# Converting a weight quarter one matmul group later: VectorE's half of the work and the reload behind it, in the last round of a routed expert layer

## The chip, the core and the metric

The kernel runs on one core of a Trainium2 chip. The metric is the device time of one execution in microseconds (us). The engines are TensorE (PE in the profile, its weight loads PEld), VectorE (DVE), ScalarE (ACT), GpSimd (POOL) and SyncE (SP), which issues most of the DMAs. A "q" behind an engine's name (DVEq) is its sequencer.

## What is computed

A Fourier transform over two axes, and then a layer of 8 experts of which each row uses one:

```python
X = np.fft.fft(np.fft.fft(x, axis=1), axis=2).real      # x: 8 x 2496 x 256
x = X.reshape(19968, 256)
logits = x @ w_gate                                     # 8 experts
e_idx = np.argmax(logits, axis=1)                       # one expert per row
gate_w = softmax(logits)[row, e_idx]
eom = sigmoid(x @ w_output_gate)
for e in range(8):
    mask = e_idx == e
    h = np.maximum(x[mask] @ w1[e], 0.0)                # 256 -> 1024
    ye = h @ w2[e]                                      # 1024 -> 256
    out[mask] = gate_w[mask, None] * eom[mask, e, None] * ye
```

Nothing is known of the routing when the kernel is built; which rows go to which expert is worked out on the chip.

## The kernel before

The transform comes first, with the gate behind it; each row is written to a scratch array `scr`, sorted by expert. Then the expert part runs over a list of slots, `sched`. Rounds 0 to 2 hold 512 rows of each expert in two slots of 256 rows, and they run while the transform of later batches goes on. The last round (`LAST`, the subject here, about 715 to 1068 us of the profiled execution) holds what is left: 27 "pair" slots of 256 rows, and 10 "single" slots of 128 rows interleaved with them. Which expert a slot of the last round has is a number in a table, read into a register when the slot comes up.

Numbers are held as sums of two 16-bit values, high and low, so each product takes three matmuls. Of a slot, four groups `g` are worked: `mm1` (line 1325, 12 matmuls into the PSUM tile `hp`, which has three buffers), then ScalarE's `hh` (line 1329, the high part of the hidden layer, and the relu), then VectorE's `hl` (line 1330, the low part, which reads `hp` and `hh`), then `mm2` of the group three earlier (line 1347, into `yp`). `hp` comes free when `hl` has read it. With `mm2` of group 2 VectorE makes `ysc` (line 1352), with that of group 3 ScalarE makes `y` (line 1355), and GpSimd scatters it (line 1356).

The weights of an expert come in four quarters: two halves of w1 (`raw0b` in 32 bit, `w0b` converted) and two of w2 (`raw1b`, `w1b`). Conversion is done by `conv`: ScalarE writes the high part (line 1300), VectorE the low part (line 1302, which reads the high one), and SyncE then issues the load of the next expert's quarter into the same raw buffer (`load_w`, line 1272, behind two register loads at line 1233). Pair slots have one set of buffers, single slots another. In the last round a pair slot whose expert is that of the slot before skips the conversion, by a branch (`tc.If`, line 1298) on a register, and skips the load's transfer by a condition on the DMA; single slots always convert.

The order on each engine is the order in which the code is written. In `experts` a slot begins with `load_x_` for the slot after next (on SyncE: `xr`, line 1255, a transposing DMA, and `xf`, line 1256). Then, for each group, `mm1`, `mm2` of the group three earlier, and conversions: the new expert's halves of w1 at groups 1 and 3 of the pair slot before it, those of w2 at groups 0 and 2 of the slot that follows. A single slot's quarters are converted from a list, `todo`, one at a time, as soon as their buffers are free.

`final` is filled when the last round's tables are ready, towards the end of round 2; from there on the order is that of the code alone.

Of the kernel before, what the change touches and what calls it, by code (L numbers as in the profile page):

```python
# [245 lines left out]
def fft_moe_kernel(ctx: ExitStack, tc: tile.TileContext, xl, wg, w1, w2, tde, tdo, gt, ts0, tsm, tsr, tsq, cst, tid, out):  # L246
# [47 lines left out]
    if True:  # L294
# [108 lines left out]
        newest, pinned, final = {}, [], []  # L403
        evacs = {}

        def behind_rows(eng, on=True):
            return tc.issue_after(evacs[eng]) if on else nullcontext()
# [773 lines left out]
    if True:  # L1181
# [25 lines left out]
        NS = len(sched)  # L1207
# [5 lines left out]
        after_new = dict(zip(news, news[1:]))  # L1213
# [3 lines left out]
        after_sing = dict(zip(sing, sing[1:]))  # L1217

        def chained(fn, n, *args):
            if n < NS:  # L1220
                fn(n, *args)
# [3 lines left out]
        def table(n):  # L1225
            rd, qi = sched[n][:2]
            return (slots_a + [slots_b, fbt])[rd], (E, NQ, NFB)[max(rd, LAST - 1) - LAST + 1], 0 if rd == FB else qi
# [56 lines left out]
        def changed(n):  # L1284

            if n not in fresh:
                t, w, qi = table(n)
                need(sched[n][0])
                fresh.clear()
                fresh[n] = nc.values_load(t[0:1, 2 * w + qi:2 * w + qi + 1], engines=CONV, min_val=0, max_val=1)  # L1290
            return fresh[n]

        def conv(n, m, h):
            rd, qi, N, wb, _, _ = sched[n]
            r, w = raw[wb][m][h], wbuf[wb][m][h]
            sc = scale_of(n, m)
            skips = wb == 0 and rd == LAST
            with tc.If(changed(n) > 0) if skips else nullcontext():  # L1298
                with behind_rows("ACT", not n):
                    nc.scalar.activation(w[:, 0], r, AF.Copy, scale=sc)  # L1300
                with behind_rows("DVE", not n):
                    nc.vector.scalar_tensor_tensor(w[:, 1], r, sc, w[:, 0], op0=ALU.mult, op1=ALU.subtract)  # L1302
            nxt = (after_new if wb == 0 else after_sing).get(n, NS)
            if n:
                chained(load_w, nxt, m, h)
            else:
                late.append((nxt, m, h))

        def halves(a, h):
            for k in ("hh", "hl"):  # L1310
                a[k, h] = fx[0].tile([128, 4, 256], F16, name=k, tag=k, bufs=3)

        def mm1(n, g):
            a = sl_[n]
            T = slice(0, a["N"])
            if g % 2 == 0:
                halves(a, g // 2)
            w1v = wbuf[a["wb"]][0][g // 2].rearrange("p a (k f) -> p a k f", k=2)
            ps = psf["h"].tile([128, 2, 256], F32, name="hp", tag="h", bufs=psf["hb"])
            for k in range(2):  # L1320
                f = 2 * g + k
                m = 0
                for kc in range(2):
                    for hl, x in ((0, kc), (0, 2 + kc), (1, kc)):
                        nc.tensor.matmul(ps[:, k, T], w1v[:, hl, kc, (f % 4) * 128:(f % 4 + 1) * 128], a["x"][:, x, T], start=(m == 0), stop=(m == 5))  # L1325
                        m += 1
            G = slice(2 * (g % 2), 2 * (g % 2) + 2)
            hh, hl = a["hh", g // 2], a["hl", g // 2]
            i = nc.scalar.activation(hh[:, G, T], ps[:, :, T], AF.Relu)  # L1329
            j = nc.vector.scalar_tensor_tensor(hl[:, G, T], ps[:, :, T], 0.0, hh[:, G, T], op0=ALU.max, op1=ALU.subtract)  # L1330
            if sched[n][0] < LAST and not final:
                newest.update(ACT=getattr(i, "ins", i), DVE=getattr(j, "ins", j))

        def mm2(n, g):
            a = sl_[n]
            U, h = a["U"], g // 2
            M = min(128, a["N"])
            w2v = wbuf[a["wb"]][1][h].rearrange("p a (f d) -> p a f d", f=4)
            if g == 0:
                a["yp"] = psf["h"].tile([128, 2, 256], F32, name="yp", tag="y", bufs=psf["yb"])  # L1340
                a["y"] = fx[0].tile([128, 2, 256], F32, name="y", tag="y", bufs=2)
                a["ys"] = fx[0].tile([128, 2], F32, name="ysc", tag="ysc", bufs=2)
            u = g % 2 if U == 2 else 0
            for f in range(4) if U == 2 else range(2 * (g % 2), 2 * (g % 2) + 2):
                for m, (k, hl) in enumerate((("hh", 0), ("hh", 1), ("hl", 0))):

                    nc.tensor.matmul(a["yp"][0:M, u], a[k, h][:, f, u * 128:u * 128 + M], w2v[:, hl, f],  # L1347
                                     start=(g == 0 and f == 0 and m == 0), stop=(h == 1 and f == 3 and m == 2), skip_group_check=U == 2)
            ys = a["ys"]
            if g == 2:  # L1350
                with behind("DVE"):
                    nc.vector.tensor_scalar(ys[:, 0:U], a["f"][:, 0:U, 0], scale_of(n, 2), None, op0=ALU.mult)
            if g == 3:
                for u in range(U):
                    nc.scalar.activation(a["y"][0:M, u], a["yp"][0:M, u], AF.Copy, scale=ys[0:M, u:u + 1])  # L1355
                    put = nc.gpsimd.indirect_dma_start(  # L1356
                        out=out[:, :], out_offset=bass.IndirectOffsetOnAxis(ap=a["f"].bitcast(I32)[0:M, u, 1:2], axis=0),
                        in_=a["y"][0:M, u], in_offset=None, bounds_check=NTOK - 1, oob_is_err=False)
                    if sched[n][0] < FB:
                        free_order("out", put)  # L1360
                del sl_[n]

        fbt = fbs = None

# [42 lines left out]
        late = []  # L1407

        def experts():
            yield "w"  # L1410
            chained(load_x_, 0)
            hold.clear()
            chained(load_x_, 1)
            for a in late:
                load_w(*a)
            yield "i"
            todo = []
            for n in range(NS + 1):
                chained(load_x_, n + 2)
                if n == sing[0] - 4:  # L1420
                    for m in range(2):
                        for h in range(2):
                            load_w(sing[0], m, h)
                if n + 3 in sing:
                    todo += [(n + 3, m, h) for m in range(2) for h in range(2)]
                for g in range(4):
                    if n < NS:
                        mm1(n, g)
                        yield "h"

                    k, j = divmod(4 * n + g - LAG, 4)
                    if 0 <= k < NS:
                        mm2(k, j)
                        yield "y"

                    nb, k_ = next_sq.get(n, (0, 0))
                    if nb:
                        for what in SQ[4 * k_ + g]:
                            if what[1] is None:
                                wscale(sched[nb][1], what[0])  # L1440
                            else:
                                wenergy(nb, *what)

                    p = n - 1 + g % 2
                    if p in next_new:
                        conv(next_new[p], (g + 1) % 2, g // 2)
                    if todo:
                        k, m, h = todo[0]

                        prev = ([-9] + sing)[sing.index(k)]  # L1450
                        if 4 * n + g >= 4 * prev + 2 * h + 1 + LAG * m:
                            conv(*todo.pop(0))
                yield ("slot", n)
            spill = nc.values_load(more[0:1, 0:1], min_val=0, max_val=1)
            with tc.If(spill > 0):  # L1455
                for n in range(NS, len(sched)):
                    load_x_(n)
                    for m in range(2):
                        for h in range(2):
                            load_w(n, m, h)  # L1460
                    for h in range(2):
                        conv(n, 0, h)
                    for g in range(4):
                        mm1(n, g)
                    for h in range(2):
                        conv(n, 1, h)
                    for g in range(4):
                        mm2(n, g)
            short = nc.values_load(more[0:1, 1:2], min_val=0, max_val=1)
            with tc.If(short > 0):  # L1470
                general()
# [40 lines left out]
    def need(i):  # L1512
        while min(i, LAST) not in ready:
            next(bg, None)
# [73 lines left out]
```

## Time and profile before

| what | value |
|---|---|
| median of three runs | 1077.16 us (1074.88 to 1079.08) |
| the profiled execution | 1077.15 us, span 1075.3 us, mean granted clock 0.987 |
| TensorE busy | 1031.2 us, 96% of the span |
| VectorE busy | 668.1 us, 62% |
| ScalarE busy | 597.5 us, 56% |
| GpSimd busy | 422.8 us, 39% |
| DMA | 170.96 MB, mean 159 GB/s |

The span is what the profile covers; 1.85 us of the profiled execution lie around it. A busy share is a mean over the transform, the early rounds and the last round, which have different limits, so for the change the stretch from 715 to 1034 us is read by itself. An instruction with a bracket at its end, as [2.13 <-DVE hl L1330], found its engine idle for so long, and was released by what stands behind the arrow. A matmul group is 12 matmuls on one line.

### The profile page before, as it was taken

To read this page: it belongs to the slowest core of one execution; us is meant where nothing else is said; L and a number is where in the kernel's file an instruction comes from. 1 tells how busy PE (TensorE), PEld (TensorE's weight loads), DVE (VectorE), ACT (ScalarE), POOL (GpSimd) and SP (SyncE) were. 2 spreads that over 40 slices of the span, in tenths; PEclk is the share of its full clock that TensorE was granted. 3 is DMA by queue.
4 is the path that set the end of the run, shared out by engine and by line. 5 is a ranking of instruction groups with operands and counts; after the bars stand their busy time and mean duration, and the time that the engine had idled before them with its cause. 6 is when DMAs were issued, how large, how long until landed. Compare 5 with 4: busy or idle time off the path is not lost. (4 is left out here: it accounts for less than half of the span.)

```text
span 1075.3 us, 27862 instructions
## 1 busy us (share of the span) xinstructions
PE 1031.2 (96%) x10179; PEld 911.9 (85%) x10179; DVE 668.1 (62%) x1381; ACT 597.5 (56%) x1099; POOL 422.8 (39%) x384
## 2 busy tenths in 40 slices
PE   8888889999999999999999999999999999999997
PEld 6676768889889889988888888888999889988996
DVE  5989787786876585566586444544535455445542
ACT  3476756776775465656544555444545555445652
POOL 0068355755574572353357752221122121212121
PEclk8998989999999999999999999999999999999999
DMA  9642565675686265566556885635737766475830
GB/s 365 204 175 83 199 167 166 194 197 138 157 206 157 76 163 141 139 168 167 145 132 172 211 206 149 158 104 139 194 74 202 167 168 131 124 202 129 194 74 24
DMA packets 152312, 170.96 MB, mean 159 GB/s; under 512 B 115309, under 2 KB 116207, under 8 KB 152164
## 3 DMA queue, kind: packets, MB, share of 16 engines
q1 hardware_dynamic: 136292, 126.48, 47.2%
q0 software_dynamic: 15728, 42.14, 11.6%
q8 instruction: 82, 1.34, 0.6%
q10 hardware_dynamic: 144, 0.46, 0.2%
q14 instruction: 66, 0.54, 0.2%
HBM read 149.45 MB, written 43.63 MB: 180 GB/s over the span
## 5 line engine op out<-in xcount | busy, mean ns | idle before, releaser
L1325 PE MATMUL hp<-xr,w0b 128*128 128x256 f16 (+2 forms) x4080 | 477.4, 267 | 8.7 <-DVE hl L1330 6.9
L1347 PE MATMUL yp<-w1b,hh 128*128 128x256 f16 x2560 | 437.9, 273 | 0.0
L1325 PEld LDWEIGHTS <-w0b 128*128 128x128 f16 x4080 | 378.6, 98 | 59.8 <-issue 13.7
L1356 POOL DMA_INDIRECT out_dram<-y,xf x160 | 181.2, 1133 | 438.9 <-ACT y L1355 390.1
L1347 PE MATMUL yp<-w1b,hl 128*128 128x256 f16 x1280 | 348.9, 273 | 0.0
L1330 DVE SCALAR_TENSOR_TENSOR hl<-hp,hh 128x512 f16<-128x512 f32 (+2 forms) x340 | 221.3, 653 | 186.1 <-ACT hh L1329 162.2
L1329 ACT ACTIVATE hh<-hp 128x512 f16<-128x512 f32 (+2 forms) x340 | 192.0, 567 | 232.1 <-PE hp L1325 229.5
L1347 PEld LDWEIGHTS <-hh 128*128 128x128 f16 x2560 | 247.3, 98 | 29.9 <-issue 0.8
L749 POOL DMA_INDIRECT scr<-rows,desti x160 | 178.5, 1115 | 186.3 <-ACT rows L746 79.1
L1347 PEld LDWEIGHTS <-hl 128*128 128x128 f16 x1280 | 125.3, 98 | 14.4
L1302 DVE SCALAR_TENSOR_TENSOR w0b<-raw0b,wsc,w0b 128x1024 f16<-128x1024 f32 x44 | 60.2, 1369 | 61.5 <-ACT w0b L1300 60.4
L1355 ACT ACTIVATE y<-yp,ysc 128x256 f32<-128x256 f32 (+1 forms) x160 | 67.6, 470 | 44.0 <-PE yp L1347 34.0
L1302 DVE SCALAR_TENSOR_TENSOR w1b<-raw1b,wsc,w1b 128x1024 f16<-128x1024 f32 x44 | 57.7, 1312 | 49.5 <-ACT w1b L1300 47.1
L1300 ACT ACTIVATE w0b<-raw0b,wsc 128x1024 f16<-128x1024 f32 x44 | 50.3, 1145 | 38.8 <-PE hp L1325 37.6
L523 PE MATMUL psb_t<-tdet,ft 128*125 128x290 f32 (+1 forms) x200 | 56.2, 433 | 10.3 <-DVE ft L480 4.4
L1300 ACT ACTIVATE w1b<-raw1b,wsc 128x1024 f16<-128x1024 f32 x44 | 50.4, 1147 | 18.7 <-PE yp L1347 12.3
L523 PEld LDWEIGHTS psb_t<-tdet,ft 128*125 128x125 f32 (+1 forms) x200 | 38.7, 200 | 25.9 <-issue 8.0
L1302 DVE SCALAR_TENSOR_TENSOR w1b<-raw1b,ssc,w1b 128x1024 f16<-128x1024 f32 x32 | 41.0, 1282 | 24.6 <-ACT w1b L1300 21.1
L1302 DVE SCALAR_TENSOR_TENSOR w0b<-raw0b,ssc,w0b 128x1024 f16<-128x1024 f32 x32 | 40.8, 1282 | 21.9 <-ACT w0b L1300 21.2
L1300 ACT ACTIVATE w0b<-raw0b,ssc 128x1024 f16<-128x1024 f32 x32 | 36.3, 1144 | 14.5 <-DMA raw0b<-in_w_dram 13.4
L1300 ACT ACTIVATE w1b<-raw1b,ssc 128x1024 f16<-128x1024 f32 x32 | 36.6, 1145 | 9.9 <-DMA raw1b<-in_w_dram 6.7
L536 DVE SCALAR_TENSOR_TENSOR alo<-psb_t,p_x,ahi 125x580 f16<-125x580 f32 (+1 forms) x40 | 32.1, 817 | 15.3 <-ACT ahi L535 15.3
(232 smaller groups left out, 954.7 us busy)
## 6 DMA issues: line engine op xcount, KB each, us to landing
raw0b<-in_w_dram SPq DMA_DIRECT2D x118, 512.0 KB
raw1b<-in_w_dram SPq DMA_DIRECT2D x118, 512.0 KB
xt<-in_xl_dram SPq DMA_DIRECT2D x40, 512.0 KB
scr<-rows,desti POOLq DMA_INDIRECT x160, 3.9
out_dram<-y,xf POOLq DMA_INDIRECT x160, 3.5
xr<-scr SPq DMA_TRANSPOSE x85
xf<-scr SPq DMA_DIRECT2D x75, 2.0 KB
tst<-in_ts_dram SPq DMA_DIRECT2D x2, 512.0 KB
```

The costliest lines, as they stand in the source:

```text
L523: nc.tensor.matmul(o[:, 0:290], ft[:, k, par, W], tdab[:, k], start=(k == 0), stop=(k == 1))
L536: nc.vector.scalar_tensor_tensor(s["alo"][W, c], ps[W, :, 0:290], sc, s["ahi"][W, c], op0=ALU.mult, op1=ALU.subtract)
L749: free_order("scr", batch=b, inst=nc.gpsimd.indirect_dma_start(out=scr[:, :], out_offset=bass.IndirectOffsetOnAxis(ap=s["desti"][:, j:j + ...
L1300: nc.scalar.activation(w[:, 0], r, AF.Copy, scale=sc)
L1302: nc.vector.scalar_tensor_tensor(w[:, 1], r, sc, w[:, 0], op0=ALU.mult, op1=ALU.subtract)
L1325: nc.tensor.matmul(ps[:, k, T], w1v[:, hl, kc, (f % 4) * 128:(f % 4 + 1) * 128], a["x"][:, x, T], start=(m == 0), stop=(m == 5))
L1329: i = nc.scalar.activation(hh[:, G, T], ps[:, :, T], AF.Relu)
L1330: j = nc.vector.scalar_tensor_tensor(hl[:, G, T], ps[:, :, T], 0.0, hh[:, G, T], op0=ALU.max, op1=ALU.subtract)
L1347: nc.tensor.matmul(a["yp"][0:M, u], a[k, h][:, f, u * 128:u * 128 + M], w2v[:, hl, f], start=(g == 0 and f == 0 and m == 0), stop=(h == 1 ...
L1355: nc.scalar.activation(a["y"][0:M, u], a["yp"][0:M, u], AF.Copy, scale=ys[0:M, u:u + 1])
L1356: put = nc.gpsimd.indirect_dma_start(out=out[:, :], out_offset=bass.IndirectOffsetOnAxis(ap=a["f"].bitcast(I32)[0:M, u, 1:2], axis=0), in_ ...
```

## The change

A conversion in the last phase (`final` is filled) of a slot of the main list is split. ScalarE's high part is issued where it was, in a branch of its own. VectorE's low part, in a second branch on the same register, and `load_w` of the next expert's quarter are put into a list, `lows`. The list is emptied right behind the next call of `mm1`, which issues that group's `mm1`, `hh` and `hl`. Before that phase, and for slots outside the main list, a conversion is issued as before.

```diff
-            with tc.If(changed(n) > 0) if skips else nullcontext():
+            def high():
                 with behind_rows("ACT", not n):
                     nc.scalar.activation(w[:, 0], r, AF.Copy, scale=sc)
+
+            def low():
                 with behind_rows("DVE", not n):
                     nc.vector.scalar_tensor_tensor(w[:, 1], r, sc, w[:, 0], op0=ALU.mult, op1=ALU.subtract)
...
+            if not final or n >= NS:
+                with tc.If(changed(n) > 0) if skips else nullcontext():
+                    high()
+                    low()
+                follow()
+                return
+            with tc.If(changed(n) > 0) if skips else nullcontext():
+                high()
+
+            def rest():
+                with tc.If(changed(n) > 0) if skips else nullcontext():
+                    low()
+                follow()
+
+            lows.append(rest)
...
+        lows = []
+
+        def flush_lows():
+            while lows:
+                lows.pop(0)()
...
                     if n < NS:
                         mm1(n, g)
+                        flush_lows()
                         yield "h"
```

`follow` is the old code that issues `load_w`. Lines behind the change are 20 higher: `hl` is line 1350, `hh` 1349, `mm1` 1345, `mm2` 1367; the low part is line 1304, the first branch 1319, the second 1323.

VectorE before, in the single slot that follows a pair slot of the last round: the first half of the next expert's w2 (`w1b_141`) between the `hl` of group 0 and that of group 1.

```order
L1330 SCALAR_TENSOR_TENSOR hl<-hp,hh 128x2x128
L1298 COMPARE_AND_BRANCH
L1302 SCALAR_TENSOR_TENSOR w1b_141<-raw1b_137,ssc,w1b_141 128x1024
L1298 UNCONDITIONAL_BRANCH x2
L1330 SCALAR_TENSOR_TENSOR hl<-hp,hh 128x2x128
L1352 TENSOR_SCALAR ysc<-xf,ssc 128x2
L1330 SCALAR_TENSOR_TENSOR hl<-hp,hh 128x2x128
```

The same place on VectorE after the change, from the branch of the second half of w1 that comes before it:

```order
L1350 SCALAR_TENSOR_TENSOR hl<-hp,hh 128x2x128
L1323 COMPARE_AND_BRANCH
L1304 SCALAR_TENSOR_TENSOR w0b_140<-raw0b_136,ssc,w0b_140 128x1024
L1323 UNCONDITIONAL_BRANCH x2
L1319 COMPARE_AND_BRANCH
L1319 UNCONDITIONAL_BRANCH x2
L1350 SCALAR_TENSOR_TENSOR hl<-hp,hh 128x2x128
L1323 COMPARE_AND_BRANCH
L1304 SCALAR_TENSOR_TENSOR w1b_141<-raw1b_137,ssc,w1b_141 128x1024
L1323 UNCONDITIONAL_BRANCH x2
L1352 TENSOR_SCALAR ysc<-xf,ssc 128x2
L1350 SCALAR_TENSOR_TENSOR hl<-hp,hh 128x2x128
```

The low part of `w1b_141` has moved behind the `hl` of group 1, and that of `w0b_140` behind the `hl` of group 0; each conversion has two branches.

SyncE before, at the same change of slot, the register work (line 1233, ISA rows and branches) left out: `raw0b_136` is the second half of w1, `raw1b_137` the first half of w2, `raw1b_10647` a quarter of a single slot.

```order
L1272 DMA raw1b_10647<-in_w_dram 128x1024
...
L1272 DMA raw0b_136<-in_w_dram 128x1024
...
L1255 DMA_TRANSPOSE xr<-scr 128x4x256
...
L1256 DMA xf<-scr 128x2x2
...
L1272 DMA raw1b_137<-in_w_dram 128x1024
```

SyncE at the same place after the change:

```order
L1272 DMA raw1b_10647<-in_w_dram 128x1024
...
L1255 DMA_TRANSPOSE xr<-scr 128x4x256
...
L1256 DMA xf<-scr 128x2x2
...
L1272 DMA raw0b_136<-in_w_dram 128x1024
...
L1272 DMA raw1b_137<-in_w_dram 128x1024
```

The load of the second half of w1 has moved behind `xr` and `xf` of the next slot; the other three quarters' loads keep their place among SyncE's DMAs.

## Rows read from the trace of the kernel before

**Rows 1.** Windows: PE, PEld, DVE, ACT, POOL busy (count), PEclk, DMA share, GB/s

```profile
800.00:900.00 100.00, 97.97 (x962) 88.29 (x960) 51.64 (x74) 50.96 (x81) 20.90 (x19) 1.00 0.64 159
900.00:1000.00 100.00, 97.86 (x961) 88.20 (x959) 51.38 (x73) 51.22 (x83) 20.38 (x19) 1.00 0.63 154
```

**Rows 2.** Waits of PE, 715 to 1034 us: total, times, longest

```profile
PE hp L1325 <- DVE hl L1330: 3.7, 2, 2.1
PE hp L1325 <- DVEq L1298: 0.4, 1, 0.4
```

**Rows 3.** Timeline of PE: start, us, instruction, [idle before <- releaser]

```profile
967.61 0.60 PE L1325 MATMUL hp<-xr,w0b 128*128 128x256 f16 x4 [2.13 <-DVE hl L1330]
```

**Rows 4.** Chain of waits, 940 to 975 us: start, us, what

```profile
959.89 4.76 DMA raw1b<-in_w_dram
...
964.76 1.16 ACT w1b L1300
...
969.74 1.31 PE hp L1325 x12
```

**Rows 5.** Timeline of DVE, same change of expert

```profile
965.94 1.28 DVE L1302 SCALAR_TENSOR_TENSOR w1b<-raw1b,ssc,w1b 128x1024 f16<-128x1024 f32 x1 [3.02 <-ACT w1b L1300]
967.14 0.42 DVE L1330 SCALAR_TENSOR_TENSOR hl<-hp,hh 128x256 f16<-128x256 f32 x1
```

**Rows 6.** Timeline of ACT, same change of expert

```profile
965.81 0.64 ACT L1329 ACTIVATE hh<-hp 128x256 f16<-128x256 f32 x2
```

**Rows 7.** Timeline of SP's DMA issues, two loads that are skipped

```profile
833.60 0.07 SPq L1272 DMA_DIRECT2D raw1b<-in_w_dram  x1
835.21 0.07 SPq L1272 DMA_DIRECT2D raw0b<-in_w_dram  x1
```

**Rows 8.** Waits of SP's queue, 760 to 975 us

```profile
SPq L1255 <- PE hp L1325: 12.5, 13, 1.9
```

**Rows 9.** Timeline of SP: second half of w1, and `xf` behind it

```profile
955.15 0.34 SPq L1272 DMA_DIRECT2D raw0b<-in_w_dram  x1
...
957.80 0.54 SPq L1256 DMA_DIRECT2D xf<-scr  x1
```

**Rows 10.** Timeline of SP: the same load at two other changes

```profile
814.30 0.33 SPq L1272 DMA_DIRECT2D raw0b<-in_w_dram  x1
...
853.38 0.34 SPq L1272 DMA_DIRECT2D raw0b<-in_w_dram  x1
```

**Rows 11.** Timeline of ACT: the conversions that wait for these two loads

```profile
820.43 1.15 ACT L1300 ACTIVATE w0b<-raw0b,ssc 128x1024 f16<-128x1024 f32 x1 [1.89 <-DMA raw0b<-in_w_dram]
...
858.76 1.15 ACT L1300 ACTIVATE w0b<-raw0b,ssc 128x1024 f16<-128x1024 f32 x1 [0.44 <-DMA raw0b<-in_w_dram]
```

**Rows 12.** Timeline of DVE: a low part of w2

```profile
830.74 1.28 DVE L1302 SCALAR_TENSOR_TENSOR w1b<-raw1b,ssc,w1b 128x1024 f16<-128x1024 f32 x1 [1.11 <-ACT w1b L1300]
```

**Rows 13.** Timeline of DVE: a change that meets a single's conversion

```profile
1009.67 2.48 DVE L1302 SCALAR_TENSOR_TENSOR w0b<-raw0b,ssc,w0b 128x1024 f16<-128x1024 f32 x2
1012.07 0.68 DVE L1330 SCALAR_TENSOR_TENSOR hl<-hp,hh 128x512 f16<-128x512 f32 x1
```

**Rows 14.** Timeline of PE: first matmuls with a new half of w1

```profile
824.29 1.47 PE L1325 MATMUL hp<-xr,w0b 128*128 128x256 f16 x12
...
1012.86 0.82 PE L1325 MATMUL hp<-xr,w0b 128*128 128x256 f16 x6
```

**Rows 15.** Branches of line 1298: count, ns min/median/max, first and last start

```profile
L1298 DVEq COMPARE_BRANCH  x132: 43/56/72, 719.5 to 1057.1; - x132
L1298 DVEq EVENT_SEMAPHORE  x84: 21/21/21, 720.1 to 1057.8; - x84
```

**Rows 16.** Timeline of DVE: low part of w1's second half

```profile
821.61 1.28 DVE L1302 SCALAR_TENSOR_TENSOR w0b<-raw0b,ssc,w0b 128x1024 f16<-128x1024 f32 x1 [2.35 <-ACT w0b L1300]
```

**Rows 17.** Waits of all engines, 715 to 1034 us

```profile
DVE hl L1330 <- ACTq L1298: 20.4, 15, 2.0
```

More of the change, by code (lines that the diff above doesn't have):

```diff
@@ L1297, in conv, with follow @@
             skips = wb == 0 and rd == LAST
-            with tc.If(changed(n) > 0) if skips else nullcontext():
+            def high():
                 with behind_rows("ACT", not n):
                     nc.scalar.activation(w[:, 0], r, AF.Copy, scale=sc)
+            def low():
                 with behind_rows("DVE", not n):
                     nc.vector.scalar_tensor_tensor(w[:, 1], r, sc, w[:, 0], op0=ALU.mult, op1=ALU.subtract)
[L1303 to L1307, printed above, removed]
+            def follow():
+                nxt = (after_new if wb == 0 else after_sing).get(n, NS)
+                if n:
+                    chained(load_w, nxt, m, h)
+                else:
+                    late.append((nxt, m, h))
+            if not final or n >= NS:
[11 more added lines that the diff above has]
+            lows.append(rest)
         def halves(a, h):
```

## The prediction, made before the changed kernel ran

> **What bounds the kernel now.** I read five views, from wide to narrow.
>
> [...]
>
> Second, TensorE's waits. From 715 to 1034 us they are 3.7 us in two pieces behind `hl` and 0.4 us in one piece behind a VectorE branch, 4.1 us in all [rows 2]. The longest, 2.13 us, ends at 967.61 [rows 3]; the other long one is then about 1.6 us. They lie at two of the six changes of expert, those with a 128-row slot behind them.
>
> Third, the chain of waits around 967.61 [rows 4]. It begins with a load: SyncE issues the first half of w2 at 959.89, and it lands 4.76 us later. ScalarE converts the high part from 964.76, VectorE the low part, then comes `hl`, and TensorE starts 0.05 us after it ends. On VectorE the low part takes 1.28 us from 965.94, and `hl` follows at 967.14 [rows 5], although the `hh` that it reads was begun at 965.81 on ScalarE, two of them in 0.64 us [rows 6]. So `hl` stands behind a low part that nothing needs yet. This is what the change turns round.
>
> Fourth, SyncE. Between changes the weight loads are skipped, but each still costs SyncE 1.61 us before the next can go: 833.60 and 835.21 [rows 7]. A full slot has four such loads, 6.4 us, plus `xr` and `xf`; TensorE takes 10.5 us for it, 8 groups of 1.31 [rows 4]. So I take SyncE to be a hidden clock: its loads go out as early as SyncE can get to them, and not when a buffer comes free. The view of SyncE's waits seems to say otherwise, with 12.5 us of `xr` behind TensorE in 13 pieces [rows 8]; that is under 1 us each, less than such a load takes on SyncE anyway (row 957.80 of `xf` comes 2.65 us behind row 955.15, with an `xr` between them [rows 9]), so I read them as its issue. I am not sure of it, and the second rival rests on the other reading.
>
> [...]
>
> **The change, part by part.**
>
> *hl ahead of the low part.* At the change near 960 us `hl` can start when the first `hh` is done: 965.81 plus half of 0.64, about 966.15. With 0.42 us for itself [rows 5] and 0.05 us to TensorE, that restarts TensorE at about 966.65 instead of 967.61: -0.96 us. The change near 860 us has the same pattern, but a gain there is not banked: what follows up to 967 us waits for SyncE's loads, whose times this does not move. The sum is therefore made at the last gap: after 967.61 TensorE does not wait again in the last round [rows 2].
>
> *The moved load.* Only the load behind the conversion at a slot's last group changes its place in SyncE's order: the second half of w1 goes behind the next slot's `xr` and `xf`. It goes out about 2.65 us later (955.15 to 957.80 [rows 9]), and the next load, w2's first half at 959.89, keeps its time. The two are then some 2.1 us apart instead of 4.7, and share the DMA. Alone, w2 took 4.76 us to land [rows 4]. For loads in crowded stretches I have two prices from issue to conversion: 853.38 to 858.76, 5.38 us, and 814.30 to 820.43, 6.13 us [rows 10, 11]. I take 5.38, that is +0.6 us, with 0 and +1.4 as ends.
>
> *SyncE's waits.* A load that follows a low part waits for a low part that is now later by up to one pair of matmul groups, 2.6 us (two of 1.31 [rows 4]). The nearest case: the low part of 830.74 ends at 832.02 [rows 12], and the load behind it goes at 833.60 [rows 7], 1.58 us later; a wait there is at most 2.6 - 1.6 = 1.0 us. One such wait lengthens the lag of all later loads, so waits do not add up. I take +0.4, ends 0 and +1.0.
>
> *Conversions that meet a single's.* Near 1010 us two low parts run on VectorE from 1009.67 in 2.48 us, and `hl` is behind them at 1012.07 [rows 13]. Turned round, `hl` would run until about 1011.9, the low part of w1's first half until 1013.2, and the matmul that needs it started at 1012.86 [rows 14]: a wait of 0.35 us, with 0 and 1.6 (the other low part goes first) as ends. It is behind the last gap, so it counts: +0.35.
>
> *Behind the change near 967.* The low part of w2, 1.28 us, now stands ahead of `ysc` and the next `hl`. TensorE has three buffers in hand, and can lose here at most what it has just gained; I take +0.3, ends 0 and +0.9.
>
> *The second branch.* There are 108 conditional conversions, of which 84 are skipped [rows 15] and 24, four at each change, are carried out; each gets a second branch, which ScalarE and VectorE must both pass. Branches take 56 ns on VectorE, and both engines are idle half the time [rows 1]; I cost them at nothing. If that cover were gone, the third rival gives the price.
>
> *Losses that are absorbed.* Near 820 us the moved load would be issued at about 817 instead of 814.30, and land between 821.8 (4.76 us) and 823.1 (6.13). Then come the high part of 1.15, `hh`, `hl` and the low part of 1.28: the half of w1 is ready between 825.2 and 826.7. Today its low part ends at 821.61 + 1.28 = 822.89 [rows 16], and the matmul that reads it starts at 824.29 [rows 14]. So TensorE waits 0.9 to 2.4 us, in the middle 1.65. Since the later gaps hold 4.1 us of waiting for SyncE, I count it as absorbed.
>
> The sum: -0.96 + 0.6 + 0.4 + 0.35 + 0.3 = +0.69 us. The profiled run took 1077.15 us (span 1075.3 and 1.85 around it), which is the median of the three runs, 1077.16; so 1077.15 + 0.69 = **1077.8 us**. With all upper ends it is -0.96 + 1.4 + 1.0 + 1.6 + 0.9 = +3.94, 1081.1 us; with all lower ends -0.96, 1076.2 us.
>
> **The rivals.**
>
> 1. *The gaps go altogether.* If `hl` is never late any more and the loads land as before, TensorE loses all of its waiting: 1077.15 - 4.1 = 1073.0 us. For it: both long waits end on `hl` by name. Against it: the chain in front of `hl` begins with a load and a ScalarE conversion, which stay.
>
> 2. *Nothing is absorbed.* If SyncE does wait for TensorE at `xr` [rows 8], a loss on TensorE moves the later loads with it. Then 1.65 us near 820 counts, and so does 0.35 us at each of the two earlier changes that meet a single's conversion: 1077.15 + 0.69 + 1.65 + 0.7 = 1080.2 us. Against it: skipped loads at an even 1.61 us.
>
> 3. *The other side: the branches cost.* VectorE's `hl` is listed as waiting for ScalarE's branch 15 times for 20.4 us in all [rows 17], 1.36 us each. If a second branch holds up ScalarE or VectorE so long once at each of the six changes, where TensorE is already out of spare buffers, that is 6 x 1.36 = 8.2 us: 1085.3 us, slower by 0.76%. It decides once a branch costs more than what VectorE has over between two groups with a conversion, 2.6 - 1.28 - 0.68 = 0.66 us [rows 12, 13]. Against it: the branch itself is 56 ns, and most of the 20.4 us are just `hl` waiting for an `hh` behind a skipped conversion.
>
> [...]
>
> 4. *It does nothing.* The order on VectorE changes, but the landing of the loads sets every restart, and the gain and the crowding cancel: 1077.2 us.
>
> **How the numbers follow.** The forecast has 0.53; the first rival 0.13, the second 0.14, the third 0.09, the fourth 0.11. What a measurement of this kernel can tell from no change is about 0.5%, 5.4 us: below 1071.8 is faster, above 1082.5 slower. Even the first rival stays inside, and going beyond it needs more idle time than TensorE has, so faster has 0.03. Slower has the third rival and a little of the second with its upper ends: 0.10. The rest, 0.87, is no change. The range takes in the first rival, the upper ends and the second: 1073.0 to 1082.0. The forecast's own is 1076.2 to 1081.1.
>
> **What would show it.** Right: near 967 us `hl` runs ahead of the low part of w2, and TensorE's last long wait is 1 to 2 us; the load of w1's second half goes out behind `xf`; near 820 us TensorE has a new wait behind the low part of w1; a small one near 1013. Wrong: TensorE without waits of over 1 us (the first rival); new waits of TensorE while the later ones stay as long as they are (the second); ScalarE or VectorE idle over 1 us around the new branch (the third). The prediction falls if the time is outside 1073 to 1082, and its reasoning falls, whatever the time, if SyncE turns out to wait for buffers instead of lagging.

## The result and the profile after

The changed kernel took 1084.49 us (median of six runs, 1082.69 to 1086.96) against 1077.02 us for the kernel before (six runs, 1074.88 to 1079.08): a ratio of 1.0068, with a 95% interval of 1.0055 to 1.0081. The forecast was 1077.8, with 1082.0 as its upper end. The change makes the kernel slower by some 7 us, and the prediction was wrong.

The profiled execution of the changed kernel has a span of 1083.0 us, 7.7 more than before. Until the last round the two run alike, but for 1.3 us: the first `hh` after 681 us begins at 681.59 before and at 682.90 after. That difference arises ahead of the last round, and varies from profile to profile: in after_again and after_3, two more of the changed kernel, the same `hh` begins at 682.12 and 683.27. Most of the rest is lost in one place. TensorE's timeline of the changed kernel shows it, with the idle time ahead of an instruction in brackets:

```profile
824.40 0.39 PE L1345 MATMUL hp<-xr,w0b 128*128 128x256 f16 x2 [3.81 <-ACT w0b L1300]
826.80 2.32 PE L1345 MATMUL hp<-xr,w0b 128*128 128x256 f16 x10 [2.01 <-DVE w0b L1304]
...
973.13 0.83 PE L1345 MATMUL hp<-xr,w0b 128*128 128x128 f16 x12 [0.71 <-DVE hl L1350]
974.97 1.25 PE L1345 MATMUL hp<-xr,w0b 128*128 128x256 f16 x10 [0.36 <-DVE hl L1350]
```

At the change of expert near 820 us, where TensorE waited for nothing before, it now waits 5.8 us inside one matmul group, the first that reads the new expert's w1: 3.8 us for the high part of the first half, and, after the two matmuls that need no more than that, 2.0 us for its low part. Near 970 us the wait of 2.13 us [rows 3] has become 0.71 and 0.36. By the grouped view of TensorE's waits it is 7.4 us where it was 4.1 [rows 2]:

```profile
PE hp L1345 <- ACT w0b L1300: 3.8, 1, 3.8
PE hp L1345 <- DVE w0b L1304: 2.0, 1, 2.0
PE hp L1345 <- DVE hl L1350: 1.1, 2, 0.7
PE yp L1367 <- DVEq L1323: 0.5, 1, 0.5
```

Waiting alone is 3.3 us more, and the last round is longer by 6.2 (its last `hh` begins 7.5 us later, less the 1.3). The windows around the wait show the other part. Their columns are those of [rows 1], and the third number from the end is the granted clock:

```profile
820.00:824.00 4.00, 0.59 (x6) 0.29 (x3) 0.00 (x0) 0.81 (x1) 0.00 (x0) 1.00 0.88 268
824.00:828.00 4.00, 1.59 (x8) 1.01 (x9) 2.48 (x3) 2.15 (x5) 1.94 (x2) 0.60 1.18 250
828.00:830.00 2.00, 2.00 (x12) 1.39 (x10) 0.00 (x0) 0.78 (x1) 0.00 (x0) 0.50 0.81 309
830.00:832.00 2.00, 2.00 (x12) 1.49 (x11) 1.11 (x2) 0.85 (x2) 0.00 (x0) 0.58 0.94 338
832.00:834.00 2.00, 2.00 (x21) 1.79 (x19) 0.77 (x1) 0.41 (x1) 0.00 (x0) 1.00 0.51 137
```

In the 4 us from 820 TensorE works 0.59 us. The clock granted to it is then 0.60 in the 4 us from 824, 0.50 and 0.58 in the two windows behind them, and 1.00 again from 832 us. In the 2 us from 828 it did 12 matmuls, in the 2 us from 832, 21. That is the rest, about 3 us: 6.2 less 3.3. The long waits of before, of 2.13 us at most, stand in windows at 1.00 [rows 1].

Why did TensorE wait? ScalarE's timeline shows that the raw quarter was not there:

```profile
823.19 1.15 ACT L1300 ACTIVATE w0b<-raw0b,ssc 128x1024 f16<-128x1024 f32 x1 [8.52 <-DMA raw0b<-in_w_dram]
829.22 1.15 ACT L1300 ACTIVATE w0b<-raw0b,ssc 128x1024 f16<-128x1024 f32 x1 [2.95 <-DMA raw0b<-in_w_dram]
```

The first row is the first half of w1, the second row the second half. VectorE shows the low parts of both, that of the first half behind an `hl` which itself waited for ScalarE:

```profile
824.86 0.69 DVE L1350 SCALAR_TENSOR_TENSOR hl<-hp,hh 128x512 f16<-128x512 f32 x1 [9.08 <-ACT hh L1349]
825.47 1.28 DVE L1304 SCALAR_TENSOR_TENSOR w0b<-raw0b,ssc,w0b 128x1024 f16<-128x1024 f32 x1
...
831.50 1.28 DVE L1304 SCALAR_TENSOR_TENSOR w0b<-raw0b,ssc,w0b 128x1024 f16<-128x1024 f32 x1
```

The first half was not there because SyncE issued it late. In SyncE's timeline the three loads in a row that begin with a single's quarter, and hold the first half of w1, stand before the change at

```profile
808.00 3.61 SPq L1272 DMA_DIRECT2D raw0b<-in_w_dram  x3
```

and after it at

```profile
816.34 3.45 SPq L1272 DMA_DIRECT2D raw0b<-in_w_dram  x3
```

That is 8.3 us later, 7.0 when the 1.3 us of the start are taken off; this is called SyncE's lag from here on. This first half of w1 is not the load that the change moved against the others: it is late because SyncE as a whole is late.

Where SyncE lost the first half of this time stands 90 us earlier. Its timeline after the change:

```profile
727.12 1.45 SPq L1255 DMA_TRANSPOSE xr<-scr  x1
732.73 0.40 SPq L1256 DMA_DIRECT2D xf<-scr  x1
```

The same two before the change:

```profile
727.06 1.91 SPq L1255 DMA_TRANSPOSE xr<-scr  x1
729.72 0.42 SPq L1256 DMA_DIRECT2D xf<-scr  x1
```

The view of SyncE's waits names what `xf` now waits for, and GpSimd's timeline has that scatter, here after the change and then before it:

```profile
SPq L1256 <- DMA out_dram<-y,xf: 3.9, 1, 3.9
```

```profile
725.54 0.97 POOL L1376 DMA_INDIRECT out_dram<-y,xf  x1 [0.30 <-ACTq L1319]
```

```profile
724.23 0.98 POOL L1356 DMA_INDIRECT out_dram<-y,xf  x1 [0.31 <-ACTq L1298]
```

`xf` has four buffers, and the scatter of an earlier slot still reads one (its row numbers come from `xf`). It was issued at 725.54 and released SyncE 7.1 us later. Before the change the load of w1's second half stood ahead of `xr` and `xf`; now these come first, SyncE stands at `xf` before the scatter has landed, and every load behind waits with it. The wait of 3.9 us has three parts: 0.5 us that `xf` waited before the change too, 1.7 us by which SyncE now comes to it earlier (the start of 1.3 us taken off), and 1.7 us by which the scatter released it later, 7.1 us after its start where it was 5.4 before. Whether that last part is the change's doing is not shown: in four other profiles with the load moved and four buffers (after_again, after_3, load_moved_3 and xf_behind, below) the same scatter took 4.8 to 7.0 us. From there on SyncE has no time to spare in this profile, and the lag stays to the end of the round. At 726 us, ahead of this wait, the lag is 1.1 us; behind it, about 3.7. By 816 us it has grown to 7.0, since some DMAs took SyncE longer to issue than the usual 1.25 us for `xr` and 0.40 for `xf`:

```profile
755.04 1.92 SPq L1255 DMA_TRANSPOSE xr<-scr  x1
...
767.25 1.28 SPq L1256 DMA_DIRECT2D xf<-scr  x1
...
793.98 2.30 SPq L1255 DMA_TRANSPOSE xr<-scr  x1
```

With one at 806.18 (1.20 for `xf`) they are 3.4 us beyond the usual from 735 to 816 us. The trace of before has one such issue there, 0.75 us too long. That accounts for most of the lag: 3.7 + 3.4 - 0.75 = 6.35, of 7.0. What makes an issue long is not settled here. Another profiled execution of the changed kernel had none in this stretch; its lag near 810 us was 2.0 us, and it took 1078.9 us.

### The profile page after: what moved, and what is told of

Its sections match the earlier page's. It is cut to its first block, busy times and chain, and to the rows that moved or that the text cites. A ratio compares the mean times of both kernels' runs of the same rounds, so it can differ in the third digit from the quotient of the medians.

```text
span 1083.0 us, 28069 instructions
## 1 busy us (share of the span) xinstructions
PE 1040.4 (96%) x10179; PEld 917.3 (85%) x10179; DVE 669.7 (62%) x1381; ACT 597.5 (55%) x1099; POOL 414.7 (38%) x384
## 5 line engine op out<-in xcount | busy, mean ns | idle before, releaser
L1376 POOL DMA_INDIRECT out_dram<-y,xf x160 | 171.6, 1073 | 455.2 <-ACT y L1375 411.4
L523 PE MATMUL psb_t<-tdet,ft 128*125 128x290 f32 (+1 forms) x200 | 61.2, 463 | 9.5 <-DVE ft L480 4.4
L523 PEld LDWEIGHTS psb_t<-tdet,ft 128*125 128x125 f32 (+1 forms) x200 | 41.7, 216 | 25.5 <-issue 8.1
L535 ACT ACTIVATE ahi<-psb_t,p_x 125x580 f16<-125x580 f32 (+1 forms) x40 | 28.9, 744 | 20.5 <-PE psb_t L523 9.8
```

Of the source, the lines that this page charges most:

```text
L523: nc.tensor.matmul(o[:, 0:290], ft[:, k, par, W], tdab[:, k], start=(k == 0), stop=(k == 1))
L535: nc.scalar.activation(s["ahi"][W, c], ps[W, :, 0:290], AF.Copy, scale=sc)
L1376: put = nc.gpsimd.indirect_dma_start(out=out[:, :], out_offset=bass.IndirectOffsetOnAxis(ap=a["f"].bitcast(I32)[0:M, u, 1:2], axis=0), in_ ...
```

## The experiments

Three theories were to be told apart. Theory A: the loss comes through SyncE, whose own time is the clock of the last round, and whose order the change has altered. Theory B: it comes from the moved load's own landing and the later low part. Theory C: the second branch costs ScalarE or VectorE. Each comparison is with the kernel before in the same set of runs. In two of the four sets, both measured on one and the same chip, the kernel before takes 1123.48 and 1121.65 us and scatters more, so that a loss of 5 us is hardly seen there.

**Is SyncE's time the clock?** Two edits take work from SyncE or add to it, and leave the order of all transfers as it is. The first makes the two register loads of `load_w` once for both halves of a weight:

```diff
+        in_regs = {}
...
-            e = entry(n, 0, 7 * 128)
+            if in_regs.get((wb, m), (None,))[0] != n:
+                in_regs[wb, m] = n, entry(n, 0, 7 * 128), entry(n, 2, 1) if wb == 0 else None
+            _, e, c = in_regs[wb, m]
             kw = {}
             if wb == 0:
-                kw["cond"] = entry(n, 2, 1)
+                kw["cond"] = c
```

On the kernel before (before_regs): 

> The kernel before, with the two register loads of a load_w made once for both halves of a weight in place of once for each quarter; nothing else. If SyncE's own time is the hidden clock of the last round (theory A), it gains some 2.5 us a slot on SyncE, the loads at the changes of expert come in time, and the 4.1 us that TensorE waits go: 3 to 5 us faster. If SyncE waits for buffers (the other reading): no change.

Measured: 1073.48 us against 1078.25, a ratio of 0.9959 (0.9946 to 0.9972). TensorE waits for nothing any more in the last round; its windows:

```profile
800.00:900.00 100.00, 100.00 (x989) 90.46 (x987) 52.77 (x76) 52.91 (x83) 20.55 (x19) 1.00 0.66 167
900.00:1000.00 100.00, 100.00 (x990) 90.48 (x989) 52.20 (x75) 52.45 (x84) 20.78 (x19) 1.00 0.64 155
```

Two skipped loads with no register work between them now go 0.65 us apart, where it was 1.61 [rows 7], and SyncE has time to wait, for scatters and for VectorE's low parts, in the stretch in which before it had at most 0.4 us at a time for these (SyncE's timeline, and its waits from 760 to 975 us):

```profile
832.01 0.07 SPq L1276 DMA_DIRECT2D raw1b<-in_w_dram  x1
832.66 0.07 SPq L1276 DMA_DIRECT2D raw0b<-in_w_dram  x1
```

```profile
SPq L1256 <- DMA out_dram<-y,xf: 15.2, 9, 5.1
SPq L1276 <- DVE w0b L1306: 10.7, 7, 2.5
SPq L1276 <- DVE w1b L1306: 8.7, 8, 2.4
```

On the changed kernel (after_regs): 

> The changed kernel with the register loads made once for both halves. Theory A: SyncE no longer lags, so the new order costs little: 1 to 5 us faster than the kernel before, and within 2 us of the kernel before with the same edit. Theory B, and the reading that SyncE waits for buffers: 5 to 7.5 us slower than before, as the changed kernel.

Measured: 1073.76 us, 0.9964 (0.9951 to 0.9977). With time on SyncE the change costs nothing that is seen (1073.76 against 1073.48 us); it gains nothing either, since no wait of TensorE is left to shorten. The second edit adds to SyncE: in `load_x_`, a second register load that nothing uses (extra_reg).

```diff
             r = entry(n, 1, DUM)
+            if rd == LAST:
+                entry(n, 1, DUM)
```

> The kernel before with one more register load on SyncE in each slot of the last round, whose value nothing uses: about 0.57 us of SyncE for each of 37 slots, 8 us by the change near 820. If SyncE's own time is the clock of the last round (theory A), 8 to 20 us slower. If SyncE waits for buffers: no change, within 1.5 us.

Measured: 1135.2 us against 1121.65, a ratio of 1.0140 (1.0084 to 1.0196), some 15 us. TensorE's waits in its profile reach 4.7 us, where two_branches_2, of the same set, has none over 1.8:

```profile
PE hp L1327 <- DVEq L1300: 8.0, 2, 4.7
PE hp L1327 <- ACT w0b L1302: 2.6, 1, 2.6
```

Half a microsecond a slot on SyncE (in the trace of before, line 1233's load takes 268 ns and the two register instructions with it 158 and 18, medians) is worth more than the whole change. This settles the clock: SyncE's own time. That the change loses through it is theory A, and after_regs speaks for it; the next edits take the change apart.

**Which part of the change?** Only the branches, with nothing moved (two_branches, two_branches_2; this cut and the next are written against the kernel before, with the change's names `high`, `low` and `follow` for its lines):

```diff
-            with tc.If(changed(n) > 0) if skips else nullcontext():
-                high()
-                low()
-            follow()
+            with tc.If(changed(n) > 0) if skips else nullcontext():
+                high()
+            with tc.If(changed(n) > 0) if skips else nullcontext():
+                low()
+            follow()
```

> The kernel before with the conversion split into two branches, nothing moved: high part, second branch, low part, load, all in the old place. Theories A and B: 1077, within 0.15%. Theory C: 1082 to 1085.

> The conversion split into two branches, nothing moved. Theory A: no change, within 1.5 us. Theory C: 5 us slower or more.

Measured: 1.0005 (0.9976 to 1.0033) and 1.0007 (0.9973 to 1.0042). No cost is seen; a cost of the size of the change's loss is outside both intervals, one of 3 us is not. In the profile of the changed kernel a branch takes 56 ns on VectorE, as before [rows 15]:

```profile
L1323 DVEq COMPARE_BRANCH  x132: 43/56/63, 722.9 to 1067.1; - x132
```

Only the load moved, the conversion where it was (load_moved, load_moved_2, load_moved_3):

```diff
             with tc.If(changed(n) > 0) if skips else nullcontext():
                 high()
                 low()
-            follow()
+            lows.append(follow)
```

> Only the load is moved behind the next group: one branch with both halves of the conversion where they were, the load from the list. SyncE's order is that of the changed kernel, VectorE's and ScalarE's that of before. Theory A: 1082 to 1085, all or nearly all of the loss. Theory B: up to half of it, 1079 to 1081. Theory C: 1077.

> Only the load moved, as before. Theory A: 3 to 7 us slower than the kernel before, most of the loss of the change. Theory C (branches): no change.

> Only the load moved. Theory A: the loss of the changed kernel, within 2 us of it. If the later low part has a share of its own: 2 to 5 us less.

Measured: 1.0034 (1.0010 to 1.0059), 1.0047 (1.0011 to 1.0083), and in the last set, the sharpest, 1.0042 (1.0027 to 1.0057): 4.5 us, of the 6.5 us of the changed kernel beside it. The load's move makes most of the loss by itself; whether the 2 us between them are a share of the later low part, the two intervals do not tell. Its `xf` is kept waiting as in the changed kernel, 3.0 us by the view of SyncE's waits:

```profile
SPq L1256 <- DMA out_dram<-y,xf: 3.0, 1, 3.0
```

The other way round, the whole change, but with `xr` and `xf` issued behind the list of the first group, which gives SyncE its old order back (x_behind, x_behind_2):

```diff
-                chained(load_x_, n + 2)
+                behind_flush = bool(final)
+                if not behind_flush:
+                    chained(load_x_, n + 2)
...
                         flush_lows()
+                        if behind_flush and g == 0:
+                            chained(load_x_, n + 2)
```

> The changed kernel, but in the last phase the rows of the slot after next (xr and xf) are issued behind the first group's list, so that on SyncE the load of w1's second half goes ahead of them again, as before the change; VectorE's order and the branches stay changed. Theory A: 1077, within 1.5. Theory B: the low part is still one group later: 1080 to 1084. Theory C: 1084.5.

> The changed kernel with xr and xf behind the first group's list, once more, beside the changed kernel itself. Theory A: 0 to 4 us faster than the kernel before, since hl is ahead of the low part and SyncE's order is the old one. Theory B: as the changed kernel, within 1 us.

Measured: 0.9967 (0.9943 to 0.9992) in the one set, 1.0013 (1.0002 to 1.0023) in the other. In that second set the changed kernel ran beside it (after_again):

> The changed kernel once more, on the chip of the three kernels beside it. Theory A (SyncE's order): it loses 5 to 7.5 us against the kernel before. Theory B (what was lost in the first comparison is one late scatter, met by chance): 0 to 3 us.

Measured: 1.0056 (1.0043 to 1.0069), with one run of five at 1078.9 and the others up to 1084.63. So the loss is no chance of the first comparison, and three quarters of it go with the old order on SyncE, with VectorE's order and the branches still changed.

**How much of it is the wait at xf?** The changed kernel with 8 buffers of `xf` in place of 4 (xf8, xf8_2, xf8_3):

```diff
-            f = a["f"] = fx[0].tile([128, 2, 2], F32, name="xf", tag="xf", bufs=4)
+            f = a["f"] = fx[0].tile([128, 2, 2], F32, name="xf", tag="xf", bufs=8)
```

> The changed kernel with 8 buffers of xf in place of 4, nothing else. Theory A (SyncE's lag): behind the moved order SyncE reaches xf so early that it waits 3.90 us for a scatter to land (728.72), and lags for the rest of the round; with more buffers that wait goes, and 3.4 us (3.90 less the 0.52 of before) come back at the change near 820: about 1081. Theory B (the landing of the moved load itself and the low part one group later cost TensorE directly): 1084.5, no change. Theory C (the second branch costs ScalarE or VectorE): 1084.5.

> The changed kernel with 8 buffers of xf, once more, on the chip of the three kernels beside it. Theory A, with the wait for the scatter at xf as its main part: that wait is some 3 us of a lag of 7, so 1 to 3 us slower than the kernel before, where the changed kernel was 5.7 to 7 us slower. If that wait is only the occasion and other steps take its place: 4 to 7 us slower.

> The changed kernel with 8 buffers of xf. If the wait for the scatter at xf is what makes SyncE late (some 3 us of its lag of 7, and with it the rest): 0 to 3 us slower than before. If SyncE is as late without it, from its other steps: 4 to 7 us slower, as the changed kernel.

and with `xf` alone issued behind the list of the first group, so that SyncE has `xr`, the load, `xf` (xf_behind):

> The changed kernel with xr where it is, but xf alone behind the list of the first group, so that on SyncE the order is xr, load of w1's second half, xf. If the wait at xf is the cause: 0 to 3 us slower than before. If the load's place behind xr is enough: 4 to 7 us slower.

```diff
-                      nc.sync.dma_start(f[:, 0:U], rows[:, D:RW].rearrange("(u p) w -> p u w", p=128))):
...
+            def load_f():
+                i = nc.sync.dma_start(f[:, 0:U], rows[:, D:RW].rearrange("(u p) w -> p u w", p=128))
...
+            if final and 3 < n < NS:
+                lows.append(load_f)
+            else:
+                load_f()
```

The changed kernel is their measure (after_3):

> The changed kernel beside the three others, as the measure for them: 5 to 7.5 us slower than the kernel before.

The first two runs of xf8 were in the sets that scatter: 0.9998 (0.9971 to 1.0026) and 1.0039 (1.0005 to 1.0072), which leaves it open. The last set decides. The changed kernel: 1084.72 us against 1077.84, 1.0060 (1.0039 to 1.0082). With 8 buffers: 1079.55 us, 1.0016 (1.0007 to 1.0025). With `xf` behind: 1081.89 us, 1.0036 (1.0024 to 1.0047). In the profile with 8 buffers `xf` goes at its time, with no wait (the same two as at 727.12 and 732.73 above):

```profile
727.39 1.31 SPq L1255 DMA_TRANSPOSE xr<-scr  x1
728.96 0.40 SPq L1256 DMA_DIRECT2D xf<-scr  x1
```

Four more buffers of 16 bytes a partition take 4.7 of the 6.5 us back. Moving `xf` alone shortens the wait to 0.9 us and takes back only 2.6 us, less than was expected of it if the wait were all. Its profile shows why: ahead of one `xr` SyncE's lag is 0.7 us and behind it 2.9, since this `xr` took 3.40 us to issue instead of 1.25:

```profile
741.12 3.40 SPq L1255 DMA_TRANSPOSE xr<-scr  x1
```

The profiles, side by side: SyncE's lag at the three loads near 810 us, and what the last round lost to the last `hh`, both against the kernel before and less the shift of the first `hh` after 681 us.

| profile | lag near 810, us | last round longer by, us |
|---|---|---|
| before | 0 | 0 |
| xf8_3 | 0.2 | 1.8 |
| x_behind_2 | 1.2 | 0.1 |
| load_moved_3 | 1.3 | 2.9 |
| after_again | 2.0 | 1.4 |
| xf_behind | 4.3 | 5.0 |
| after_3 | 5.2 | 6.4 |
| after | 7.0 | 6.2 |

Above 4 us of lag the loss is 5 to 6.4 us; at 2.0 and below it is 0.1 to 2.9, and doesn't follow the lag. Near 825 us the granted clock is down to 0.60 and then 0.50 in after, and to 0.64 and then 0.87 in after_3. Over the whole execution its mean is 0.977 and 0.982 in these two, and 0.987 before; xf_behind loses its 5.0 us at 0.988. In all but before and x_behind_2 the moved load itself goes another 2 to 3 us later than the loads beside it, and x_behind_2 is the one that loses next to nothing; so a part of what is lost at a small lag may be theory B's. No run tells this apart.

## Why the prediction was wrong

*The bound was named rightly, and its consequence missed.* The prediction took SyncE as a hidden clock of the last round. The register edits show that it is, in both directions. The other reading, that SyncE waits for TensorE at `xr` [rows 8], is out for the kernel before: with 124 of SyncE's 284 register loads away, the first thing that happened was that SyncE began to wait elsewhere, and TensorE stopped waiting. The trace of before says it too. `xr` has three buffers, and each `xr` of the last round starts 2.3 us or more behind the `hh` of the last group that read its buffer; even the longest, 2.35 us at 871.00, has its buffer free since 867.35.

*The step that failed is "SyncE's waits": +0.4, with 0 and +1.0 as ends.* It counted the waits of a load for its later low part, and in this it was not far off: the lag from them is 1.1 us at 726 us. It did not count the wait of the instructions that the load was moved behind. `xr` and `xf` come earlier by one load, and `xf` had a wait of its own, for the landing of a scatter. It was in the trace of before, ahead of `xf` at 729.72, in a view of which the prediction shows only the part from 760 us on (SyncE's waits, 715 to 760 us, before the change):

```profile
SPq L1256 <- DMA out_dram<-y,xf: 0.5, 1, 0.5
```

Since `xf` already waited 0.5 us, all of its advance, 1.7 us, became more waiting. SyncE's lag, which is what the term prices, was 7.0 us near 810 in the profile, not 0.4: 1.1 from the low part, 2.6 more behind the wait at `xf`, and most of the rest from long issues, of which after_again, with a lag of 2.0, had none. With 8 buffers of `xf` the lag there is 0.2 us and the kernel loses 1.7 us (0.8 to 2.7), not far from the +0.69 of the sum.

*"Losses that are absorbed" fell with it.* Near 820 us TensorE waited 5.8 us, against 0.9 to 2.4 forecast, and not for the half that the forecast names. All of it is for the first half of w1, whose load SyncE issued late and whose low part stood behind an `hl`. The low part of the second half was done at 831.50 + 1.28 = 832.78, ahead of the group that reads it, at 834.19. The forecast wait is there in after_again, where SyncE lags by 2.0 us: 0.85 us for the first half's low part and then 1.06 for that of the second (TensorE's timeline):

```profile
820.88 1.27 PE L1345 MATMUL hp<-xr,w0b 128*128 128x256 f16 x10 [0.85 <-DVE w0b L1304]
...
827.35 1.27 PE L1345 MATMUL hp<-xr,w0b 128*128 128x256 f16 x10 [1.06 <-DVE w0b L1304]
```

Absorption itself worked as described, but could not pay: the later waits shrank from 4.1 us to 1.6, since TensorE was late as well, while SyncE's later loads stayed as late as the lag made them. And a price was missing: after the wait, the lower clock cost about 3 us, as much again as the net waiting.

*The term -0.96 was right in kind.* Near 970 us `hl` now runs ahead of the low part of w2, on VectorE's timeline of the changed kernel, where before it stood behind [rows 5]:

```profile
974.50 0.42 DVE L1350 SCALAR_TENSOR_TENSOR hl<-hp,hh 128x256 f16<-128x256 f32 x1 [0.23 <-ACT hh L1349]
974.84 1.28 DVE L1304 SCALAR_TENSOR_TENSOR w1b<-raw1b,ssc,w1b 128x1024 f16<-128x1024 f32 x1
```

TensorE's wait is shorter there by 1.06 us, 2.13 less 0.71 and 0.36. How much of that is the order and how much TensorE's own lateness, the profile does not tell. The order also has a price that the term +0.3 behind it does not name: `mm2` reads the low part of w2, which now comes later. TensorE waits at `yp` for that low part or its branch 0.5 us in the changed kernel's profile and 1.7 to 2.1 us in the five others of the table with the low part moved, and not at all in before and load_moved_3; two_branches_2, with nothing moved, has 1.5 us of it.

*The moved load's crowding, +0.6, did not come.* It went out behind `xf`, as foreseen, and w2's first half 1.85 us later:

```profile
964.50 0.40 SPq L1256 DMA_DIRECT2D xf<-scr  x1
966.45 0.33 SPq L1272 DMA_DIRECT2D raw0b<-in_w_dram  x1
968.30 0.33 SPq L1272 DMA_DIRECT2D raw1b<-in_w_dram  x1
```

Both were ready for ScalarE within 4.75 us of their issue, as ScalarE's timeline shows, where one alone had taken 4.76 [rows 4]:

```profile
971.20 1.15 ACT L1300 ACTIVATE w0b<-raw0b,ssc 128x1024 f16<-128x1024 f32 x1 [3.30 <-DMA raw0b<-in_w_dram]
972.25 0.36 ACT L1349 ACTIVATE hh<-hp 128x256 f16<-128x256 f32 x1
973.04 1.15 ACT L1300 ACTIVATE w1b<-raw1b,ssc 128x1024 f16<-128x1024 f32 x1 [0.43 <-DMA raw1b<-in_w_dram]
```

*The wait of 0.35 near 1013 did not come either*: after 974.97 TensorE waits for nothing in the last round. The second branch at nothing agrees with the two runs, within their 3 us.

*The rivals.* The third was nearest, 1085.3 us against 1084.49, and on the right side, but by luck: no run speaks for its mechanism, the cost of the branches. The second, nothing absorbed, 1080.2 us, had SyncE wait for TensorE, which it does not do. The gap-free kernel of the first rival, 1073.0 us, exists: it is the kernel before with the register loads made once, 1073.48 us.

Issuing was the clock of the round, although a load that is carried out takes longer to land, 4.76 us [rows 4], than to issue, 0.34 us [rows 9]: a skipped one has nothing to move and costs SyncE 1.61 us [rows 7], of which 0.65 are left without its register loads. With that time given back, SyncE waits for scatters, 15.2 us from 760 to 975 us in before_regs, and for VectorE's low parts, 19.4 us.

What stays open is what makes single issues of `xr` and `xf` on SyncE two or three times as long as usual (2.30 and 3.40 us where 1.25 is usual, 1.28 where 0.40 is), why one scatter held its buffer for 4.8 to 7.1 us, and so why the lag of one and the same kernel near 810 us was 2.0, 5.2 and 7.0 us in three profiles.

## What to carry to other kernels

When an engine that issues DMAs has no idle time, as SyncE here, look for the critical path on it: one register load more in each slot made this kernel some 15 us slower, and a skipped transfer still cost SyncE 1.61 us [rows 7], so count its register loads before its bytes. When a step moves past others on a queue, look up each of these others in the view of waits: what now comes earlier may wait for its buffer, as `xf` did here for 3.9 us, and what stands behind it waits as well: SyncE's lag went from 1.1 us to 3.7 there. Here the reorder cost 6.5 us, four small buffers gave 4.7 of them back, and making the register loads of `load_w` half as often made the kernel 4.4 us faster than it was before.

## What was not expected of the hardware

One wait of TensorE of 5.8 us in two pieces was followed by a granted clock of 0.50 to 0.60 from 824 to 832 us, while waits of 1.6 and 2.13 us, with full work around them, left the clock of their 100-us windows at 1.00 [rows 1]; the ten matmuls behind the wait of 2.01 us took 2.32 us, those behind 0.85 and 1.06 us in after_again 1.27 each. A load that is skipped by its condition took SyncE 1.61 us [rows 7], and 0.65 us without its register loads. A scatter that takes GpSimd 0.97 us to issue held its buffer for 7.1 us from its start, and 5.4 us in the kernel before.
